# Products of k and v in column halves, one run of forty a batch, in a linear-attention, gated-attention and MLP kernel

## The chip, the cores and the metric

The kernel runs on one core of one Trainium2 chip. The metric is device time in microseconds of one execution; the kernel before was run three times. Its engines are named as in the profile: PE (TensorE), DVE (VectorE), ACT (ScalarE), POOL (GpSimd), SP (the queue that issues most DMAs).

## What is computed

Three stages follow one another for 8 batches of 576 positions, in f32. The change is in the first, a linear attention with 8 heads of 64 columns and a root-mean-square norm:

```python
kv = np.einsum('bhsd,bhse->bhde', k, v)
out = np.einsum('bhsd,bhde->bhse', q, kv)
rms = np.sqrt(np.mean(out * out, axis=-1, keepdims=True) + 1e-06)
return (out / rms * g_norm).astype(np.float32)
```

Its output, 512 wide, is the input x of the second stage: 4 experts of 64 columns, of which a gate picks two for each position. Each expert takes `q = x @ wq[e]`, `k = x @ wk[e]`, `v = x @ wv[e]`, causal softmax scores, `a @ v @ wo[e]`. The third stage is an MLP with a gelu, a layer norm and a product over positions:

```python
h = x @ w_in
h = 0.5 * h * (1.0 + np.tanh(c * (h + 0.044715 * h ** 3)))
...
v_s = np.einsum('ts,bsd->btd', w_sg, v_n) + b_sg[None, :, None]
gated = u * v_s
return (x + gated @ w_out).astype(np.float32)
```

## The kernel before

**Stages.** `Phase1` holds the first two stages, `Phase2` the MLP. For each batch `b`, Phase1 has six streams of work, each a generator:

- `front(b)`, the linear attention. Heads are handled in four pairs `c`, 128 columns wide. `kv` multiplies all 128 columns of k of a pair with all 128 of v, over five blocks of positions (three of 128, two of 96), into a PSUM bank `kvps`; the two 64x64 blocks on the diagonal are the heads' own, and ACT (upper) and DVE (lower) copy these into one of two f32 tiles `bd`, which were set to zero once. `outT` multiplies `bd` with q (two halves of 288 positions, `outps`); ACT copies the result to `o32` (named `o` in the trace) and POOL squares it (`sq`); in batch 0 DVE copies and ACT squares. `stat` sums the squares by head (`statps`, four column strips of 32), `rstd` makes the inverse root from it: ACT writes `ya` with a logarithm and an exponential, DVE refines it (`yb`, `yc`, `ya`), ACT and DVE split it (`yh`, `rr`).
- `normall(b)`: PE spreads `rr` over the columns (`nps`), DVE scales `o`, ACT rounds it to `xhi`, and DVE or POOL takes the rest `xlo`.
- `vpart(b)` (`vps`) and `qkpart(0, b)`, `qkpart(1, b)` (`qkps`): products with the weights, each in three terms of high and low parts.
- `attn(b)`: scores (`scps`), softmax (`prob`), transposes (`tps`, copied to `aT`), the product with v (`avps`, in two column halves of 64, `rps`), and its split `gav`, `gvh`, `gvl`.

Two more streams convert the MLP's weights (`cv_...` on DVE, ACT and POOL, and `wxps` on PE) and, at the start, split the weights of the projections (`wstage` into `whi` by ACT and `wlo` by POOL).

**Tiles.** In PSUM, four banks belong to `attn` (`psa`), three to all the rest of Phase1 (`psp`), one to `statps`. k, v and q of one pair are one load: three DMAs into a tile pair of the pool `ld`, which has `ldb` = 2 buffers; the loads of pairs 2 and 3 of batch 0 go to borrowed tiles (`kvmore`, `qmore`). `front` issues the load that takes a buffer over as soon as `kv` is recorded.

**The order.** The functions do not issue instructions; `Recorder` notes them. `merge` interleaves the streams: `OPT["w"]` gives each stream a start and an end in units of batches, and the number after each `yield` says how much of the stream is then done. `Recorder.plan` plays the recorded operations through a model of the engines, in which every engine takes the first ready operation in the merged order; `LAG` says how long a signal takes from one engine to another. `trace` then issues all operations in the order of their planned starts, all from line 453, so every row of the profile has that line. `together(ops)` marks matmuls that the plan must keep adjacent, and spreads their planned cost over the column tiles.

```python
def front(self, b, st):
    ...
    for c in range(NC):
        ops = self.kv(b, c)
        if b or c < 2:
            self.load(b * NC + c + (OPT["ldb"] if b else 2 + OPT["ldb"]))
        yield 1.1
        with self.hp("o"):
            sqs.append(self.outT(b, c, st, ops))
```

Of the kernel before, what the change touches and what calls it, by code (L numbers as in the profile page):

```python
# [27 lines left out]
F32 = mybir.dt.float32  # L28
F32R = mybir.dt.float32r
# [9 lines left out]
P = 128  # L39
S = 576  # L40
# [3 lines left out]
NC = 4  # L44
NQ = 5
HF = 288
BIG = 1.0e9
SMALL = float(np.array(897 << 20, np.uint32).view(np.float32))
OPT = dict(ob=1, sx=0, pinq=0, dv=0, pin=1, cvb=2, xb=1, ldb=2, hp={}, n1=0, n2=0, f1=0, pa=4, sA=(), dg=0, cost=(1.01, 0.88, 1.22, 1.47, 1.28), avi=1, prb=4, ahb=4, alb=2, qkb=2, ahead=3, w={'attn': (0.177, 1.304), 'qk1': (0.052, 0.235), 'qk0': (-0.558, 0.001), 'v': (-0.498, -0.304), 'front': (-1.553, -1.195), 'norm': (-0.834, -0.735), 'conv': (-0.409, 3.651), 'conv2': (3.099, 6.937), 'wts': (-1.719, -1.216), 'u': (-0.111, 1.169), 'front_0': (-1.826, -1.644), 'v_0': (-1.188, -0.934), 'qk0_0': (-1.196, -1.087), 'qk1_0': (0.028, 0.513), 'norm_0': (-1.552, -1.457)})

# [11 lines left out]
def _rows(i):  # L62

    return P if i < 3 else 96
# [5 lines left out]

LAG = {"tensor": 0.12, "vector": 0.13, "scalar": 0.13, "gpsimd": 0.13, "sync": 0.25, "dma": 0.12}
MODE = 0.15
# [389 lines left out]
class Phase1:  # L462
# [31 lines left out]
    def first_loads(self):  # L494

        nc = self.nc
        more = self.at.tile([P, 2, 2, NQ, P], F32, name="kvmore", tag="more", bufs=1)
        for n in range(NC):
            if n < 2:
                self.load(n)  # L500
            else:
                q = self.at.tile([P, S], F32, name="qmore", tag="prob", bufs=OPT["prb"])
                self.load(n, more[:, n - 2], q)
        for n in range(NC, NC + OPT["ldb"] - 2):
            self.load(n)
        self.stg = []
        for n0, n1 in ((512, 772), (0, 256), (256, 512)):
            st = self.staging(NC * (n1 - n0)).rearrange("p (c n) -> p c n", c=NC)
            nc.sync.dma_start(st, self.wqkvg.rearrange("(c p) n -> p c n", p=P)[:, :, n0:n1])
            self.stg.append(st)  # L510
# [4 lines left out]

    def load(self, n, kv=None, q=None):
        b, c = divmod(n, NC)
        if b >= self.nb:
            return
        nc = self.nc  # L520
        if kv is None:
            kv = self.ld.tile([P, 2, NQ, P], F32, name="kv", tag="kv")
            q = self.ld.tile([P, S], F32, name="q", tag="q")
        src = self.kvp[b, c]
        nc.sync.dma_start(kv[:, :, 0:3, :], src[:, 0:384].rearrange("t (p j) d -> p t (j d)", j=3))
        nc.sync.dma_start(kv[:96, :, 3:5, :], src[:, 384:S].rearrange("t (p j) d -> p t (j d)", j=2))
        nc.sync.dma_start(q, self.qT[b, c * P : (c + 1) * P, :])
        self.loads[n] = (q, kv[:, 0], kv[:, 1])

    def consts(self):  # L530
        nc, cst = self.nc, self.cst
# [12 lines left out]
        for j in range(E - 1):  # L544
            nc.gpsimd.memset(self.tri[:, :, j, j + 1 : E], 1.0)
        self.bd = []
        for i in range(2):
            t = cst.tile([P, P], F32, name=f"bd{i}")
            nc.vector.memset(t, 0.0)
            self.bd.append(t)  # L550
        self.rr = cst.tile([P, HF], F32R, name="rr")
# [31 lines left out]

    def kv(self, b, c):
        nc = self.nc
        q, k, v = self.loads[b * NC + c]
        ps = self.bank("kvps")
        for j in range(NQ):
            n = _rows(j)
            nc.tensor.matmul(ps[:, 0:P], k[:n, j, :], v[:n, j, :], start=(j == 0), stop=(j == NQ - 1))  # L590
        bd = self.bd[c % 2]
        nc.scalar.copy(bd[0:64, 0:64], ps[0:64, 0:64])
        nc.vector.tensor_copy(bd[64:128, 64:128], ps[64:128, 64:128])
        return bd, q

    def outT(self, b, c, st, ops):

        nc = self.nc
        bd, q = ops
        sq = self.tmp.tile([P, S], F32, name="sq", tag="sq", bufs=NC)  # L600
        for h in range(2):
            r = slice(HF * h, HF * (h + 1))
            ps = self.bank("outps")[:, 0:HF]
# [6 lines left out]
        if b:  # L610
            o = st["o32"][:, c, :]
# [17 lines left out]
    def rstd(self, st):  # L629
        nc = self.nc  # L630
# [7 lines left out]
        nc.vector.scalar_tensor_tensor(y, a, 1.5, y, op0=OP.add, op1=OP.mult)  # L638
        yh = self.tmp.tile([P, HF], F32R, name="yh", tag="yd")
        nc.scalar.copy(yh, y)  # L640
# [98 lines left out]
    def front(self, b, st):  # L739
# [4 lines left out]
        sqs = []  # L744
        for c in range(NC):
            ops = self.kv(b, c)
            if b or c < 2:
                self.load(b * NC + c + (OPT["ldb"] if b else 2 + OPT["ldb"]))
            yield 1.1
            with self.hp("o"):  # L750
                sqs.append(self.outT(b, c, st, ops))
            yield 0.75
            if c > 0:
                yield 0.5
        self.stat(st, sqs)
# [267 lines left out]
    def streams(self):  # L1023
# [4 lines left out]
        for b in range(self.nb):  # L1028
            st = sts[b]
            for name, gen, total, out in (  # L1030
# [4 lines left out]
                ("norm", self.normall(b, st), 1.0, prep),  # L1035
                ("front", self.front(b, st), 9.4, prep),
            ):
# [405 lines left out]
```

## Time and profile before

| | us |
|---|---|
| median of three runs | 847.2 (846.85 to 847.46) |
| the profiled execution | 847.4 |
| its span on the core | 845.6 |
| PE, DVE, ACT, POOL busy in it | 811.3, 462.3, 398.0, 321.9 |

A busy share counts the time in which at least one instruction of the engine is in work. PE's matmuls overlap and their ends are modelled, so what a matmul costs is the distance from its start to the next one's, which the chain of waits gives: it follows the execution back from its last instruction, at each step to what released it or to the instruction ahead of it on its engine. Waits are listed by who waited for whom. A matmul in f32 stands as two instructions in the trace, and as one in the order of a built program.

### The profile page before, as it was taken

How to read it: one execution, taken by the hardware profiler on the slowest of the kernel's cores; microseconds unless marked ns; L12 is line 12 of the kernel's file. 1: busy time of each engine (PE TensorE's matmuls, PEld its weight loads, DVE VectorE, ACT ScalarE, POOL GpSimd, SP SyncE). 2: the span in 40 equal slices, each digit the busy share in tenths (PEclk: the TensorE clock that was granted, in tenths of full speed). 3: DMA queues.
4: the chain of work that ended last, by engine and by line, in shares of the span. 5: the costliest groups of instructions: out<-in, count | busy, mean ns of one | idle time of the engine just before them, and what ended most of it. 6: DMA issues, size and time to landing. Idle time of an engine off the chain costs nothing.

```text
span 845.6 us, 15457 instructions
## 1 busy us (share of the span) xinstructions
PE 811.3 (96%) x5496; PEld 722.2 (85%) x5496; DVE 462.3 (55%) x1274; ACT 398.0 (47%) x1048; POOL 321.9 (38%) x387
## 2 busy tenths in 40 slices
PE   6599999999999999999999699999999999999998
PEld 5498979889798898888987599898989899898996
DVE  2557567776664757868656767362544435341330
ACT  3446466575565666667666673422333223322110
POOL 1963645647343343886311424131213222120120
PEclk9699999999999999999999899999999999999999
DMA  9667757687567777856379380302102030101011
GB/s 303 185 190 200 200 142 206 173 216 214 145 180 198 188 202 216 229 157 166 96 181 307 122 289 1 105 2 102 30 26 81 26 106 13 38 13 51 14 38 63
DMA packets 77088, 114.42 MB, mean 135 GB/s; under 512 B 13265, under 2 KB 40593, under 8 KB 77010
## 3 DMA queue, kind: packets, MB, share of 16 engines
q1 hardware_dynamic: 76866, 112.90, 46.2%
q8 instruction: 44, 0.72, 0.4%
q0 software_dynamic: 144, 0.52, 0.2%
q14 instruction: 34, 0.28, 0.1%
HBM read 58.31 MB, written 26.77 MB: 101 GB/s over the span
## 4 chain that ended last, share of the span: by engine, by line
PE 84%; DVE 7%; POOL 3%; ACT 3%; issue 2%; DMA 1%; SPq 0%; ACTq 0%; POOLq 0%; DVEq 0%
PE ps L453 42%; PE qkps L453 10%; PE vps L453 7%; PE scps L453 5%; PE tps L453 4%; PE avps L453 4%; PE kvps L453 4%; PE outps L453 4%; PE wxps L453 2%; PE nps L453 1%; DVE ya L453 1%; DVE yb L453 1%; DVE prob L453 1%; DMA q<-in_qT 1%; PE statps L453 1%
## 5 line engine op out<-in xcount | busy, mean ns | idle before, releaser
L453 PE MATMUL ps<-wsh,vn 128*128 128x288 f32 x576 | 120.1, 295 | 0.0
L453 ACT ACTIVATE prob<-prob,small 128x128 f32<-128x128 f32 (+4 forms) x160 | 96.5, 604 | 33.2 <-DVE small L453 29.7
L453 PEld LDWEIGHTS ps<-wsh,vn 128*128 128x128 f32 x576 | 94.3, 188 | 0.6
L453 POOL TENSOR_TENSOR gl<-g,gh 128x512 fp32r<-128x512 f32 x32 | 41.2, 1288 | 140.4 <-ACT gh L453 140.4
L453 PE MATMUL qkps<-xhi,whi 128*128 128x288 f32 x256 | 78.8, 308 | 1.4 <-DVE o L453 1.4
L453 DVE CUSTOM_DVE_ANT_0 prob<-scps,mask_sb 128x128 f32<-128x128 f32 (+4 forms) x160 | 73.8, 474 | 6.1 <-PE scps L453 5.3
L453 PE MATMUL qkps<-xlo,whi 128*128 128x288 f32 x256 | 77.0, 301 | 0.0
L453 PE MATMUL qkps<-xhi,wlo 128*128 128x288 f32 x256 | 76.6, 299 | 0.0
L453 PE MATMUL ps<-wsl,vn 128*128 128x288 f32 x256 | 75.5, 295 | 0.0
L453 PE MATMUL tps<-id_sb,prob 96*128 96x96 f32 (+2 forms) x480 | 71.2, 259 | 3.6 <-ACT aT L453 2.6
L453 PE MATMUL scps<-kh,qs 128*128 128x128 f32 (+2 forms) x192 | 67.3, 355 | 4.0 <-DVE aT L453 2.1
L453 POOL TENSOR_SCALAR lny<-mv 128x1 f32<-128x1 f32 x36 | 24.3, 674 | 120.5 <-DVE mv L453 120.4
L453 PE MATMUL scps<-kl,qs 128*128 128x128 f32 (+2 forms) x192 | 59.8, 314 | 0.0
L453 PEld LDWEIGHTS tps<-id_sb,prob 96*128 96x128 f32 (+2 forms) x480 | 52.0, 139 | 8.7 <-ACT aT L453 3.6
L453 ACT CAST gh<-g 128x512 fp32r<-128x512 f32 x32 | 19.9, 621 | 78.6 <-DVE g L453 60.9
L453 POOL TENSOR_TENSOR xlo<-o,xhi 128x576 fp32r<-128x576 f32 (+1 forms) x32 | 42.9, 1352 | 34.1 <-ACT xhi L453 27.3
L453 DVE TENSOR_TENSOR g<-ps,u 128x288 f32<-128x288 f32 x64 | 28.6, 451 | 41.9 <-PE ps L453 41.9
L453 PEld LDWEIGHTS qkps<-xhi,whi 128*128 128x128 f32 x256 | 48.7, 190 | 2.4 <-issue 1.7
L453 PE MATMUL ps<-wo2h,gl 128*128 128x512 f32 x128 | 50.1, 391 | 0.0
L453 PE MATMUL ps<-wo2l,gh 128*128 128x512 f32 x128 | 50.0, 391 | 0.0
L453 PE MATMUL ps<-wo2h,gh 128*128 128x512 f32 x128 | 49.9, 390 | 0.0
L453 PEld LDWEIGHTS qkps<-xlo,whi 128*128 128x128 f32 x256 | 48.9, 191 | 0.4
(174 smaller groups left out, 2214.1 us busy)
## 6 DMA issues: line engine op xcount, KB each, us to landing
kv<-in_kvp SPq DMA_DIRECT2D x30, 384.0 KB, 4.6
kh<-hiT SPq DMA_DIRECT2D x64, 144.0 KB, 2.9
kl<-loT SPq DMA_DIRECT2D x64, 144.0 KB, 2.9
q<-in_qT SPq DMA_DIRECT2D x30, 288.0 KB, 4.2
out<-oev SPq DMA_DIRECT2D x32, 256.0 KB, 2.0
kv<-in_kvp SPq DMA_DIRECT2D x30, 192.0 KB, 4.8
qs<-hiT SPq DMA_DIRECT2D x32, 144.0 KB, 2.5
qs<-loT SPq DMA_DIRECT2D x32, 144.0 KB, 2.6
```

The lines of the kernel that those rows point to most:

```text
L453: f(*[val(v) for v in op.args], **{k: val(v) for k, v in op.kw.items()})
```

## The change

- `kv(b, cs)` works on a list of pairs. It makes one product for each head: 64 columns of k by 64 of v, written to partitions 0 to 63 or 64 to 127 of the same columns of one bank. For four pairs that is 40 matmuls, and `together` keeps them adjacent. One ACT copy and one DVE copy move the blocks of all pairs in the list into one tile `bd` of four blocks.
- `front` calls it with all four pairs, but in batch 0 pair by pair. A load follows each `outT`, four pairs ahead.
- `ldb` is 4; the borrowed tiles and the special case in `first_loads` are gone; `yh` shares `yb`'s buffer.
- `LAG` is 0.2 us for PE, DVE, ACT and POOL, and several windows of `OPT["w"]` have other numbers. Both move the planned order everywhere in Phase1.

```diff
-LAG = {"tensor": 0.12, "vector": 0.13, "scalar": 0.13, "gpsimd": 0.13, "sync": 0.25, "dma": 0.12}
+LAG = {"tensor": 0.2, "vector": 0.2, "scalar": 0.2, "gpsimd": 0.2, "sync": 0.25, "dma": 0.12}
...
-        more = self.at.tile([P, 2, 2, NQ, P], F32, name="kvmore", tag="more", bufs=1)
-        for n in range(NC):
-            if n < 2:
-                self.load(n)
-            else:
-                q = self.at.tile([P, S], F32, name="qmore", tag="prob", bufs=OPT["prb"])
-                self.load(n, more[:, n - 2], q)
-        for n in range(NC, NC + OPT["ldb"] - 2):
+        for n in range(OPT["ldb"]):
             self.load(n)
...
-        self.bd = []
-        for i in range(2):
-            t = cst.tile([P, P], F32, name=f"bd{i}")
-            nc.vector.memset(t, 0.0)
-            self.bd.append(t)
+        self.bd = cst.tile([P, NC, P], F32, name="bd")
+        nc.vector.memset(self.bd, 0.0)
...
-    def kv(self, b, c):
-        nc = self.nc
-        q, k, v = self.loads[b * NC + c]
-        ps = self.bank("kvps")
-        for j in range(NQ):
-            n = _rows(j)
-            nc.tensor.matmul(ps[:, 0:P], k[:n, j, :], v[:n, j, :], start=(j == 0), stop=(j == NQ - 1))
-        bd = self.bd[c % 2]
-        nc.scalar.copy(bd[0:64, 0:64], ps[0:64, 0:64])
-        nc.vector.tensor_copy(bd[64:128, 64:128], ps[64:128, 64:128])
-        return bd, q
+    def kv(self, b, cs):
+        nc = self.nc
+        ps = self.bank("kvps")[:, 0:256].rearrange("p (c d) -> p c d", c=NC)
+        ops = []
+        for c in cs:
+            _, k, v = self.loads[b * NC + c]
+            for j in range(NQ):
+                n = _rows(j)
+                for r in (slice(0, 64), slice(64, 128)):
+                    ops.append(nc.tensor.matmul(ps[r, c], k[:n, j, r], v[:n, j, r], start=(j == 0), stop=(j == NQ - 1)))
+        nc.together(ops)
+        r = slice(cs[0], cs[-1] + 1)
+        nc.scalar.copy(self.bd[0:64, r, 0:64], ps[0:64, r])
+        nc.vector.tensor_copy(self.bd[64:128, r, 64:128], ps[64:128, r])
...
-        yh = self.tmp.tile([P, HF], F32R, name="yh", tag="yd")
+        yh = self.tmp.tile([P, HF], F32R, name="yh", tag="yb")
...
-        for c in range(NC):
-            ops = self.kv(b, c)
-            if b or c < 2:
-                self.load(b * NC + c + (OPT["ldb"] if b else 2 + OPT["ldb"]))
-            yield 1.1
-            with self.hp("o"):
-                sqs.append(self.outT(b, c, st, ops))
-            yield 0.75
-            if c > 0:
-                yield 0.5
+        for cs in [(c,) for c in range(NC)] if b == 0 else [range(NC)]:
+            self.kv(b, cs)
+            yield 0.6 * len(cs)
+            for c in cs:
+                sqs.append(self.outT(b, c, st))
+                self.load(b * NC + c + OPT["ldb"])
+                yield 1.0
```

In the `OPT` line `ldb=2` becomes `ldb=4`, and of the windows, `qk0`, `v`, `conv`, `conv2`, `wts`, `u` and those of batch 0 are moved by up to 0.3 of a batch. The weights after `front`'s yields change with its steps, and its total in `streams` from 9.4 to 6.9.

What the planned order makes of it, at three places. A row is an instruction with its output and inputs, "x40" forty alike in a row; a number behind a name is that of a buffer.

**PE inside a batch of the attention stage.** Before, at the first product of a batch's `kv`:

```order
L453 MATMUL qkps<-xhi,wlo 128x288
L453 MATMUL kvps<-kv 128x128 x5
L453 MATMUL tps<-id_sb,prob 128x96 x4
L453 MATMUL tps<-id_sb,prob 96x96
L453 MATMUL scps<-kh_2308,qs_1962 96x512
L453 MATMUL scps<-kl_2320,qs_1962 96x512
L453 MATMUL outps<-q,bd_87 128x288 x2
L453 MATMUL vps<-whi,xhi 128x260
```

After, at the same place:

```order
L453 MATMUL scps<-kh_2264,qs_2045 128x384
L453 MATMUL scps<-kl_2272,qs_2045 128x384
L453 MATMUL kvps<-kv 64x64 x40
L453 MATMUL tps<-id_sb,prob 128x96 x4
L453 MATMUL tps<-id_sb,prob 96x96
L453 MATMUL scps<-kh_2264,qs_2045 96x512
L453 MATMUL scps<-kl_2272,qs_2045 96x512
L453 MATMUL vps<-whi,xhi 128x260
```

The five matmuls of the first pair are replaced by the forty of all four; the three other groups of five, which stood further on between `vps` and `qkps` work, are gone, and the first `outps` has moved further back.

**ACT and DVE in the start.** ACT before, from the last pair of batch 0 on (`whi` are the casts of the projections' weights, `sq` the squares):

```order
L453 ACTIVATE sq<-outps 128x288 x2
L453 COPY bd_89<-kvps 64x64
L453 ACTIVATE sq<-outps 128x288 x2
L453 CAST whi<-wstage 128x260 x4
L453 CAST whi<-wstage 128x256 x7
L453 ACTIVATE ya<-statps,eps 128x288
L453 ACTIVATE ya<-ya 128x288
L453 CAST whi<-wstage 128x256
L453 COPY bd_87<-kvps 64x64
L453 CAST yh<-ya 128x288
```

ACT after:

```order
L453 ACTIVATE sq<-outps 128x288 x2
L453 COPY bd<-kvps 64x64
L453 CAST whi<-wstage 128x260 x4
L453 ACTIVATE sq<-outps 128x288 x2
L453 CAST whi<-wstage 128x256 x7
L453 ACTIVATE ya<-statps,eps 128x288
L453 ACTIVATE ya<-ya 128x288
L453 CAST whi<-wstage 128x256
L453 CAST yh<-ya 128x288
```

The four casts of the first part now stand ahead of the last pair's squares, and the copy of a batch 1 block between the last cast and `yh` is gone. DVE before, from that block's copy on:

```order
L453 COPY bd_87<-kvps 64x64
L453 TENSOR_SCALAR yc<-ya,side 128x288
L453 SCALAR_TENSOR_TENSOR rr<-yh,side,yc 128x288
L453 SCALAR_TENSOR_TENSOR o_164<-o_164,g_sb,nps 128x288 x2
L453 TENSOR_TENSOR xlo<-o_164,xhi 128x288
L453 SCALAR_TENSOR_TENSOR o_164<-o_164,g_sb,nps 128x288
L453 TENSOR_SCALAR cv_x_332<-cv_w 128x256
L453 SCALAR_TENSOR_TENSOR o_164<-o_164,g_sb,nps 128x288
L453 SCALAR_TENSOR_TENSOR cv_h<-cv_w,cv_x_332 128x256
L453 TENSOR_TENSOR xlo<-o_164,xhi 128x288
L453 SCALAR_TENSOR_TENSOR o_164<-o_164,g_sb,nps 128x288 x2
L453 TENSOR_SCALAR cv_h<-cv_x_332 128x256
```

DVE after, from the refined `ya` on:

```order
L453 SCALAR_TENSOR_TENSOR ya<-yb,ya 128x288
L453 TENSOR_SCALAR yc<-ya,side 128x288
L453 SCALAR_TENSOR_TENSOR rr<-yh,side,yc 128x288
L453 SCALAR_TENSOR_TENSOR o_168<-o_168,g_sb,nps 128x288 x3
L453 TENSOR_TENSOR xlo<-o_168,xhi 128x288
L453 SCALAR_TENSOR_TENSOR o_168<-o_168,g_sb,nps 128x288 x2
L453 TENSOR_TENSOR xlo<-o_168,xhi 128x288
L453 SCALAR_TENSOR_TENSOR o_168<-o_168,g_sb,nps 128x288 x2
L453 TENSOR_TENSOR xlo<-o_168,xhi 128x288
L453 SCALAR_TENSOR_TENSOR o_168<-o_168,g_sb,nps 128x288
L453 TENSOR_SCALAR cv_x_382<-cv_w 128x256
L453 TENSOR_TENSOR xlo<-o_168,xhi 128x288
```

The copy to `bd` is gone, and the conversion steps (`cv_x`, `cv_h`) that stood between the eight scalings of `o` stand behind them.

**DVE around `rstd` of a later batch.** `ISA prob` is the masked row minimum of scores, `ISA small` its read-out. Before, from the row sums on:

```order
L453 TENSOR_SCALAR yb<-statps 128x288
L453 TENSOR_TENSOR gav<-gav,rps 128x256
L453 TENSOR_TENSOR gav<-gav,rps 128x320
L453 TENSOR_TENSOR yc<-ya 128x288
L453 SCALAR_TENSOR_TENSOR yb<-yc,yb 128x288
L453 ISA prob,small<-scps,mask_sb 128x128
L453 ISA small 128x1
L453 SCALAR_TENSOR_TENSOR ya<-yb,ya 128x288
L453 TENSOR_TENSOR loT<-qkps,hiT 128x288
L453 TENSOR_SCALAR yc<-ya,side 128x288
L453 COPY aT_2261<-tps 128x3x128
L453 SCALAR_TENSOR_TENSOR rr<-yh,side,yc 128x288
```

After:

```order
L453 TENSOR_SCALAR yb<-statps 128x288
L453 TENSOR_TENSOR gav<-gav,rps 128x256
L453 TENSOR_TENSOR gav<-gav,rps 128x320
L453 TENSOR_TENSOR yc<-ya 128x288
L453 ISA prob,small<-scps,mask_sb 128x128
L453 ISA small 128x1
L453 SCALAR_TENSOR_TENSOR yb<-yc,yb 128x288
L453 COPY aT_2331<-tps 128x3x128
L453 SCALAR_TENSOR_TENSOR ya<-yb,ya 128x288
L453 ISA prob,small<-scps,mask_sb 128x256
L453 ISA small 128x1
L453 TENSOR_SCALAR yc<-ya,side 128x288
```

The two steps that refine `yb` and `ya` now have an `aT` copy between them, so that this copy stands ahead of `ya` in place of behind it; the copy of `loT` that stood there is elsewhere.

## Rows read from the trace of the kernel before

**Rows 1.** The page: busy time, share of the span and instructions of each engine.

```profile
PE 811.3 (96%) x5496; PEld 722.2 (85%) x5496; DVE 462.3 (55%) x1274; ACT 398.0 (47%) x1048; POOL 321.9 (38%) x387
```

**Rows 2.** Stretches of the span, PE alone: us, PE busy, granted clock, DMA share, GB/s.

```profile
0.00:40.00 40.00, 23.94 (x105) 0.83 0.83 251
...
330.00:385.00 55.00, 53.17 (x416) 1.00 0.67 186
...
500.00:846.00 346.00, 341.83 (x1981) 1.00 0.15 48
...
26.40:43.50 17.10, 11.78 (x39) 0.50 0.46 131
```

**Rows 3.** PE's waits: who for whom, us in total, times, longest us.

```profile
PE tps L453 <- ACT aT L453: 2.6, 4, 0.7
PE scps L453 <- DVE aT L453: 2.1, 3, 0.9
```

**Rows 4.** Chain that ended last, batches 3 and 4: start us, us, what.

```profile
154.20 1.14 PE kvps L453 x10
...
157.41 0.97 PE outps L453 x4
...
160.03 2.91 PE avps L453 x28
162.94 1.15 PE statps L453 x16
...
190.81 1.11 PE kvps L453 x10
```

**Rows 5.** Timeline near 126 us, PE; then PE's groups by form (last column: idle).

```profile
125.77 0.66 PE L453 MATMUL avps<-aT,vst 96*64 96x192 f32 x8
...
L453 PE MATMUL avps<-aT,vst 96*64 96x96 f32 x64 | 5.7, 245 | 0.0
```

**Rows 6.** Stretch with the most PE instructions in 2.3 us, columns as in rows 2.

```profile
378.80:381.10 2.30, 2.30 (x32) 1.00 0.03 7
```

**Rows 7.** Timeline of the start, PE: start us, us, instruction, count, [idle before <-releaser].

```profile
21.71 1.35 PE L453 MATMUL kvps<-kv 128*128 128x128 f32 x10 [0.20 <-PE statps L453]
29.72 1.33 PE L453 MATMUL outps<-q,bd 128*128 128x288 f32 x2 [6.65 <-DVE bd L453]
...
38.70 0.58 PE L453 MATMUL qkps<-xhi,whi 128*128 128x288 f32 x1 [1.38 <-DVE o L453]
```

**Rows 8.** Start: ACT, POOL timelines; loads of wstage (ns, first and last start, landing).

```profile
17.83 0.21 ACT L453 COPY bd<-kvps 64x64 f32<-64x64 f32 x1 [0.76 <-PE kvps L453]
...
19.93 1.33 ACT L453 CAST whi<-wstage 128x260 fp32r<-128x260 f32 x4
...
20.48 0.73 POOL L453 TENSOR_TENSOR wlo<-wstage,whi 128x260 fp32r<-128x260 f32 x1 [17.79 <-ACT whi L453]
...
L453 SPq DMA_DIRECT2D wstage<-in_wqkvg x3: 368/378/379, 9.4 to 11.5; - x3
...
DMA to landing us min/median/max: 7.5/8.3/8.7
```

**Rows 9.** Timeline of the start, DVE and (last row) ACT, as rows 7.

```profile
29.43 0.23 DVE L453 COPY bd<-kvps 64x64 f32<-64x64 f32 x1 [0.22 <-ACT bd L453]
...
31.90 0.99 DVE L453 SCALAR_TENSOR_TENSOR o<-o,g_sb,nps 128x288 f32<-128x288 f32 x2 [0.94 <-PE nps L453]
...
38.05 0.93 DVE L453 SCALAR_TENSOR_TENSOR o<-o,g_sb,nps 128x288 f32<-128x288 f32 x2
...
41.25 0.40 ACT L453 COPY o<-outps 128x288 f32<-128x288 f32 x1 [1.81 <-POOL xlo L453]
```

**Rows 10.** Timelines of DVE and PE in batch 4; eight ya by tile, min/median/max ns.

```profile
222.41 1.53 DVE L453 SCALAR_TENSOR_TENSOR ya<-yb,ya 128x288 f32<-128x288 f32 x1
...
224.84 0.38 PE L453 MATMUL tps<-id_sb,prob 96*128 96x96 f32 x2 [0.75 <-ACT aT L453]
...
L453 DVE SCALAR_TENSOR_TENSOR ya<-yb,ya x8: 459/1397/1531, 28.8 to 385.0; 128x288 f32<-128x288 f32 x8
```

More of the change, by code (lines that the diff above doesn't have):

```diff
@@ L48 @@
 SMALL = float(np.array(897 << 20, np.uint32).view(np.float32))
-OPT = dict(ob=1, sx=0, pinq=0, dv=0, pin=1, cvb=2, xb=1, ldb=2, hp={}, n1=0, n2=0, f1=0, pa=4, sA=(), dg=0, cost=(1.01, 0.88, 1.22, 1.47, 1.28), avi=1, prb=4, ahb=4, alb=2, qkb=2, ahead=3, w={'attn': (0.177, 1.304), 'qk1': (0.052, 0.235), 'qk0': (-0.558, 0.001), 'v': (-0.498, -0.304), 'front': (-1.553, -1.195), 'norm': (-0.834, -0.735), 'conv': (-0.409, 3.651), 'conv2': (3.099, 6.937), 'wts': (-1.719, -1.216), 'u': (-0.111, 1.169), 'front_0': (-1.826, -1.644), 'v_0': (-1.188, -0.934), 'qk0_0': (-1.196, -1.087), 'qk1_0': (0.028, 0.513), 'norm_0': (-1.552, -1.457)})
+OPT = dict(ob=1, sx=0, pinq=0, dv=0, pin=1, cvb=2, xb=1, ldb=4, hp={}, n1=0, n2=0, f1=0, pa=4, sA=(), dg=0, cost=(1.01, 0.88, 1.22, 1.47, 1.28), avi=1, prb=4, ahb=4, alb=2, qkb=2, ahead=3, w={'attn': (0.177, 1.304), 'qk1': (0.052, 0.235), 'qk0': (-0.631, -0.034), 'v': (-0.498, -0.468), 'front': (-1.553, -1.195), 'norm': (-0.834, -0.735), 'conv': (-0.532, 3.653), 'conv2': (2.801, 6.802), 'wts': (-1.719, -1.234), 'u': (-0.339, 0.941), 'front_0': (-1.733, -1.703), 'v_0': (-1.21, -0.923), 'qk0_0': (-1.183, -0.856), 'qk1_0': (0.099, 0.394), 'norm_0': (-1.303, -1.273)})
 AFTER = {
@@ L514, in staging, with load @@
         return self.at.tile([P, n], F32, name="wstage", tag="aT1", bufs=OPT["ahb"])
-    def load(self, n, kv=None, q=None):
+    def load(self, n):
         b, c = divmod(n, NC)
@@ L520, in load @@
         nc = self.nc
-        if kv is None:
-            kv = self.ld.tile([P, 2, NQ, P], F32, name="kv", tag="kv")
-            q = self.ld.tile([P, S], F32, name="q", tag="q")
+        kv = self.ld.tile([P, 2, NQ, P], F32, name="kv", tag="kv")
+        q = self.ld.tile([P, S], F32, name="q", tag="q")
         src = self.kvp[b, c]
@@ L581, in hp, with outT @@
         return self.tc.high_priority(offset=n) if n else nullcontext()
-    def kv(self, b, c):
+    def kv(self, b, cs):
         nc = self.nc
-        q, k, v = self.loads[b * NC + c]
-        ps = self.bank("kvps")
-        for j in range(NQ):
-            n = _rows(j)
-            nc.tensor.matmul(ps[:, 0:P], k[:n, j, :], v[:n, j, :], start=(j == 0), stop=(j == NQ - 1))
-        bd = self.bd[c % 2]
-        nc.scalar.copy(bd[0:64, 0:64], ps[0:64, 0:64])
-        nc.vector.tensor_copy(bd[64:128, 64:128], ps[64:128, 64:128])
-        return bd, q
-    def outT(self, b, c, st, ops):
+        ps = self.bank("kvps")[:, 0:256].rearrange("p (c d) -> p c d", c=NC)
[10 more added lines that the diff above has]
+        nc.vector.tensor_copy(self.bd[64:128, r, 64:128], ps[64:128, r])
+    def outT(self, b, c, st):
         nc = self.nc
-        bd, q = ops
+        bd, q = self.bd[:, c, :], self.loads[b * NC + c][0]
         sq = self.tmp.tile([P, S], F32, name="sq", tag="sq", bufs=NC)
@@ L1035, in streams @@
                 ("norm", self.normall(b, st), 1.0, prep),
-                ("front", self.front(b, st), 9.4, prep),
+                ("front", self.front(b, st), 6.9, prep),
             ):
```

## The prediction

> **What bounds the kernel now.** I began with the page: TensorE (PE) is busy for 96% of the span [rows 1]. A busy PE need not be a PE at its peak, so the second view was the stretches. In the attention stage one batch takes 55 us, and even the loosest of these stretches has PE busy for all but 1.8 us, at the full granted clock; the long last stretch is busy for 98%. The first 40 us are different: 23.9 us busy, and part of them at half the clock [rows 2]. The third view, PE's waits, shows what recurs behind the start: a small wait, once a batch, on copies of transposed scores [rows 3]. So from 40 to 455 us an edit pays by what it takes off PE's own queue; before that, by what it takes off the chain of the other engines. The stage behind the attention is not touched.
>
> **The products of k and v.** The fourth view is the chain of waits. Each pair of heads costs PE ten matmul instructions in 1.11 to 1.14 us (five blocks of rows, two passes each for f32), four times a batch: 4.49 us [rows 4]. Half of what they compute, the blocks that mix two heads, is thrown away.
>
> After the change a step is two 64-column halves that write different partitions; there are forty such steps a batch (20 blocks of rows by two passes), in one run. To price a step I take two sizes from the chain [rows 4]: four instructions of 288 columns in 0.97 us (0.2425 each), ten of 128 in 1.11 (0.111 each). The line through them is 5.8 ns plus 0.822 ns a column, so 64 columns take 58.4 ns. That the halves run side by side is seen in the attention product, whose 28 instructions work in the same column halves: each half streams 2 x 1632 = 3264 columns, by the line 2.76 us, and the row says 2.91 us for both halves together [rows 4]. The rest, 0.15 us, is the turn into and out of this way of working; the row sums, in four column strips, leave 1.15 - 0.97 = 0.18. I take 0.17. The block then costs 40 x 0.0584 + 0.17 = 2.51 us in place of 4.49: **-1.98 us a batch**.
>
> The line is proven down to 96 columns: the last eight instructions of the attention product (two steps of 192, one of 96, then the last pair's own 0.245) take 0.66 us, so 0.415 for 480 columns, where the line says 0.412 [rows 5]. What no row shows is 64. Bounds: at best the line; next, a step that goes no faster than the 96-column one (0.082 us, so 3.45 us a block, a gain of 1.04); at worst the two halves go one behind the other (0.117 us, 4.85 us, a loss of 0.36). I take the line, since its 96-column point is nearest and loads two halves of 64 columns already.
>
> One thing else is new: 80 instructions in 2.3 us, 29 ns each. The densest 2.3 us that I found holds 32, 72 ns each [rows 6], and these were set by their columns, not by how fast they came. [...] The sum stays with the line.
>
> Batches 2 to 7 have the full gain: 6 x 1.98 = **-11.9**. Batch 1 has less, because one of its four products stands at 21.71 us today, and half of one product with q at 29.72, both in time that PE idles anyway [rows 7]; now all stand in the dense stretch. Before: 3 x 1.12 = 3.36; after: 2.51 + 2 x 0.2425 = 3.00; **-0.4**. Batch 0 is in the start, below. The copies of the blocks fall from four a batch on each of ACT and DVE to one wide one: worth nothing, as neither engine bounds. A block now waits for the last of its four loads. Its buffer comes free with the last product of the batch before with q, which ends at 158.4 us where the next batch's products begin at 190.81 [rows 4]: 32 us of cover, against 8.7 us for the slowest landing in [rows 8]. If it went, each us late would be a us of PE.
>
> **The start, 20 to 39 us.** PE's dense work begins at 38.70 us, released by DVE [rows 7], and the chain back from there runs through POOL's splitting of the weights, which began at 20.48 when ACT had cast their first part, at 19.93 [rows 8]. ACT's casts stood behind two squares of the last pair. The new order has the casts ahead of these. The weights' first part lands at 9.4 + 7.5 = 16.9 us at the earliest, and the copy ahead of the casts ends at 18.04 [rows 8]. So POOL starts between 17.5 (the landing decides) and 18.6 (the copy stays where it is): -1.9 to -3.0. I take -2.3, since shorter products bring the copy forward a little. The same POOL and ACT instructions then follow up to rr, all earlier by that. Next, the copies of a batch 1 block leave the queues between ya and rr: DVE's alone is 0.22 us idle and 0.23 work [rows 9]; -0.4. Then, from the first o (31.90) to the one that released PE (about 38.52), DVE needed 6.6 us for seven o, three xlo and four conversion steps [rows 9]. In the new order no conversion step stands among the first eight o. And a PSUM bank of batch 1, held until ACT's copy at 41.25 [rows 9], is free, so three banks turn over in place of two and the sixth o is enough: six o and two xlo, an xlo (same width) priced as an o, 8 x 0.465 = 3.7, so -2.9. Sum -5.6. Against it stands the clock: PE idled from 23.1 us [rows 7] and had the lower level, 1.2 GHz, from 26.4 to 43.5 us [rows 2]; the idle stretch begins earlier now, and each us of dense work at that level costs half a us. I take **-5.0**, bounds -1.5 (a gate that I missed, conversions late elsewhere) and -6.5.
>
> **The stall once a batch.** At 222.41 DVE's ya takes 1.53 us beside POOL's gvl; the shortest of the eight takes 0.46 [rows 10]. Behind it in DVE's queue stand loT, yc and the copy aT, and PE's next transposes wait 0.75 us. Seven such waits sum to 4.7 us (2.6 + 2.1) [rows 3]. The new order puts one aT copy ahead of ya. What follows ya can still be late, so I take two thirds: **-3.0**, bounds 0 and -4.7. The wider allowances for signals (0.2 us for 0.12 and 0.13) and the new windows move the rest of the lists; PE has 1 to 1.8 us of idle time a batch, most of it this stall, so I give them no term, but up to -4 in the range.
>
> **The sum.** The profiled execution took 847.4 us, 0.2 above the median. 847.4 - 11.9 - 0.4 - 5.0 - 3.0 = 827.1; forecast 827 us.
>
> **Rivals.**
> - *The halves overlap in part*: steps of 0.082 us. Batches 2 to 7 gain 6.2, batch 1 loses 0.6 (3.45 + 0.49 - 3.36), start and stall as above: 833.8. For it: nothing shorter than 96 columns is in the trace. Against: the line fits there to 3 ns in 415.
> - *The change does not do what it says*: halves one behind the other, 0.117 us a step. 6 x 0.36 + 2.0 lost, 8.0 gained: 843.6. Against it: the 2.91 us of [rows 4].
> - *Instructions come too slowly*: PE takes them no faster than its densest stretch shows, 72 ns. A block costs 80 x 0.072 + 0.17 = 5.9; six batches lose 1.4 each, batch 1 loses 3.1; with 8.0 gained elsewhere 851, **slower**. It decides from 65 ns an instruction, where 560 of these instructions eat all gains. For it: no row shows a faster run of that length. Against: the stretch in [rows 6] had columns to stream all the time. [...]
>
> **How the numbers follow.** Forecast 0.65 (its own bounds 820 to 834: start at -6.5, the whole stall and the 4 us; or start at -1.5 and no stall gain), partial overlap 0.18 (834 to 841 in the same way), one behind the other 0.08, too slow 0.06, and 0.03 for a new wait of another kind. The range 820 to 841 leaves out the last three, 0.17. A measurement can tell about 0.2% (1.7 us) from no change. Faster: 0.65 + 0.18 + most of 0.08; what is left of that and a part of the slow cases count as the same. That gives 0.88, 0.05, 0.07.
>
> **What would show it.** Right: the chain of waits has one block of 80 kvps instructions of about 2.3 us a batch; the first dense PE row stands near 33 to 34 us; from one block to the next it is about 53 us where it is 55; the stretch behind the change of stage is as long as now (some 346 us). Wrong: kvps blocks of 3.3 us or more; POOL's first wlo still at 20 us; a wait of PE on kv loads or on bd; transposes still waiting 0.7 us on aT; or a longer change of stage.

## The result and the profile after

The changed kernel takes **826.27 us** (median of 4 runs, 825.42 to 828.0), the kernel before 847.33 us in the same comparison: a ratio of 0.9754, 95% interval 0.9735 to 0.9773. The forecast was 827.0, the range 820 to 841. The profiled execution took 827.08 us with a span of 825.2; the span before was 845.6, so 20.4 us are to be placed.

The page and three stretches of PE, for [rows 1, 2] (us, PE busy, granted clock, DMA share, GB/s):

```profile
PE 796.0 (96%) x5816; PEld 702.6 (85%) x5816; DVE 453.5 (55%) x1252; ACT 395.1 (48%) x1027; POOL 323.7 (39%) x387
```

```profile
34.00:40.00 6.00, 5.50 (x44) 1.00 0.32 93
280.00:332.00 52.00, 51.41 (x465) 1.00 0.81 217
500.00:825.00 325.00, 321.42 (x1846) 1.00 0.14 46
```

PE's share is 96% as before. A kernel can become 20 us shorter with its bound as busy as it was: there was less for PE to do, and the rest moved up. The first row is the start: PE already works at full clock (1.00) where the kernel before had the half clock (0.50) [rows 2].

**The block.** The chain of waits, batch 3, for [rows 4] (start us, us, what):

```profile
127.63 2.48 PE kvps L453 x80
...
181.83 2.48 PE kvps L453 x80
```

All seven blocks read 2.48 us. Such a row goes from the end of the group ahead to the end of the group itself, not from start to start, as the section on the time before has it. What a block costs is seen only together with its neighbours, in the timeline of PE (start us, us, instruction, count; a duration runs into the next row, as 49.05 + 0.29 is past 49.27):

```profile
49.05 0.29 PE L453 MATMUL qkps<-xhi,wlo 128*128 128x288 f32 x1
49.27 2.55 PE L453 MATMUL kvps<-kv 128*64 128x64 f32 x80
51.75 0.40 PE L453 MATMUL qkps<-xhi,whi 128*128 128x288 f32 x1
51.99 0.29 PE L453 MATMUL qkps<-xlo,whi 128*128 128x288 f32 x1
```

Two such qkps elsewhere follow each other by 0.13 (48.92 and 49.05, for one). Here the block starts 0.22 after the one ahead of it, and the one behind it takes 0.24 to its successor. From 49.05 to 51.99 are 2.94; less 0.13 for each of the two qkps, the block costs PE 2.68. The seven blocks give 2.62 to 2.68 in this way, 2.65 in the mean. The kernel before, two of the four pairs of batch 3:

```profile
135.38 1.28 PE L453 MATMUL kvps<-kv 128*128 128x128 f32 x10
136.49 0.49 PE L453 MATMUL tps<-id_sb,prob 96*128 96x96 f32 x4
...
154.03 1.31 PE L453 MATMUL kvps<-kv 128*128 128x128 f32 x10
155.09 0.38 PE L453 MATMUL qkps<-xhi,whi 128*128 128x288 f32 x1
155.31 0.29 PE L453 MATMUL qkps<-xlo,whi 128*128 128x288 f32 x1
```

From start to start these pairs read 1.11 and 1.06. But the qkps behind the second one takes 0.22 to its successor, where 0.13 is usual, and these 0.09 belong to the pair: 1.15. In this way the four pairs add up to the 4.49 of the chain's rows [rows 4]. A block costs PE 1.84 less than the four pairs.

**The waits of PE** on work of the attention stage, first of the changed kernel (100 to 420 us), then of the kernel before (105 to 420 us); in total, times, longest:

```profile
PE scps L453 <- DVE small L453: 1.2, 4, 0.5
PE outps L453 <- DVE loT L453: 0.6, 1, 0.6
PE scps L453 <- DVE aT L453: 0.3, 1, 0.3
PE qkps L453 <- DVE o L453: 0.2, 1, 0.2
```

```profile
PE tps L453 <- ACT aT L453: 2.6, 4, 0.7
PE scps L453 <- DVE aT L453: 1.9, 2, 0.9
PE scps L453 <- DVE gav L453: 0.9, 2, 0.5
PE tps L453 <- DVE small L453: 0.4, 2, 0.2
PE tps L453 <- DVE aT L453: 0.4, 1, 0.4
```

2.3 us in place of 6.2. The waits on aT are all but gone. From the first dense row of PE to its last avps, before and after (columns as in the stretches above):

```profile
38.70:471.60 432.90, 425.30 (x3288) 0.99 0.69 191
34.91:452.54 417.63, 413.34 (x3584) 1.00 0.73 197
```

Over this whole part of the execution PE idles for 4.3 us in place of 7.6.

**The start**, timelines of the changed kernel (PE, ACT, POOL and DVE; in brackets the idle time before and who ended it):

```profile
15.53 2.29 PE L453 MATMUL outps<-q,bd 128*128 128x288 f32 x4 [0.57 <-DVE bd L453]
...
19.24 1.34 ACT L453 CAST whi<-wstage 128x260 fp32r<-128x260 f32 x4
...
19.79 1.42 POOL L453 TENSOR_TENSOR wlo<-wstage,whi 128x260 fp32r<-128x260 f32 x2 [17.10 <-ACT whi L453]
...
31.13 1.48 DVE L453 SCALAR_TENSOR_TENSOR o<-o,g_sb,nps 128x288 f32<-128x288 f32 x3 [0.96 <-PE nps L453]
...
34.27 0.93 DVE L453 SCALAR_TENSOR_TENSOR o<-o,g_sb,nps 128x288 f32<-128x288 f32 x2
...
34.91 0.36 PE L453 MATMUL vps<-whi,xhi 128*128 128x260 f32 x1 [0.50 <-DVE o L453]
```

The dense work begins at 34.91 in place of 38.70 us, but POOL's first wlo at 19.79 in place of 20.48 [rows 7, 8]: the start is shorter, in part by other steps than forecast. The first o begins at 31.13 in place of 31.90 [rows 9], and the sixth, which released PE, ends near 34.8: 3.6 us of DVE, where it took 6.6 before.

**Sum of the profiles.** The dense work begins 3.8 us earlier, the part up to the last avps is 15.3 shorter (417.6 in place of 432.9), and the rest up to the end 1.3 (372.7 in place of 374.0). Of the 15.3, the blocks of batches 2 to 7 are 6 x (4.49 - 2.65) = 11.0 and the idle time 3.3. The kernel before ran its dense work at half the clock from 38.70 to 43.5 us [rows 2, 7], the changed kernel none of it: half of 4.8 is another 2.4 (an estimate). Batch 1 gives 0.2 by the forecast's reckoning with 2.65 for the block. Against it stand 0.9 us for four products of the MLP (`ps`) that now come ahead of the last avps; that work is missing from the rest. These come to 16.0; 0.7 stays open.

| us | forecast | measured |
|---|---|---|
| blocks of batches 2 to 7 | -11.9 | -11.0 |
| batch 1 | -0.4 | -0.2 |
| the start with its clock | -5.0 | -3.8 - 2.4 = -6.2 |
| idle time in the attention | -3.0 | -3.3 |
| the rest | 0 | -1.3 + 0.9 = -0.4 |
| sum | -20.3 | -21.1; the spans differ by -20.4 |

### The profile page after: what moved, and what is told of

Its sections match the earlier page's. It is cut to its first block, busy times and chain, and to the rows that moved or that the text cites. A ratio compares the mean times of both kernels' runs of the same rounds, so it can differ in the third digit from the quotient of the medians.

```text
span 825.2 us, 16042 instructions
## 1 busy us (share of the span) xinstructions
PE 796.0 (96%) x5816; PEld 702.6 (85%) x5816; DVE 453.5 (55%) x1252; ACT 395.1 (48%) x1027; POOL 323.7 (39%) x387
## 4 chain that ended last, share of the span: by engine, by line
PE 84%; DVE 6%; DMA 4%; ACT 2%; issue 2%; SPq 1%; POOL 1%; DVEq 0%; ACTq 0%; POOLq 0%
PE ps L453 43%; PE qkps L453 10%; PE vps L453 7%; PE scps L453 5%; PE avps L453 5%; PE outps L453 4%; PE tps L453 4%; PE kvps L453 3%; PE wxps L453 2%; DMA xl<-gvl 1%; PE nps L453 1%; SPq L453 1%; PE statps L453 1%; DMA wsl<-wd1l 1%; DMA q<-in_qT 1%
## 5 line engine op out<-in xcount | busy, mean ns | idle before, releaser
L453 DVE CUSTOM_DVE_ANT_0 prob<-scps,mask_sb 128x128 f32<-128x128 f32 (+4 forms) x160 | 74.8, 475 | 10.5 <-PE scps L453 9.5
L453 ACT ACTIVATE vn<-vg,lny 128x512 fp32r<-128x512 f32 x32 | 23.1, 725 | 57.1 <-POOL lny L453 55.6
```

Of the source, the lines that this page charges most:

```text
L453: f(*[val(v) for v in op.args], **{k: val(v) for k, v in op.kw.items()})
```

## The experiments

The first question was whether the halves carry the gain, or the new order list.

**Full width again, still adjacent.** The order of all other instructions is that of the changed kernel.

```diff
+        if b > 0:
+            return self.kv_full(b, cs)
...
+                ops.append(nc.tensor.matmul(ps[:, c], k[:n, j, :], v[:n, j, :], start=(j == 0), stop=(j == NQ - 1)))
```

> The changed kernel, with the products of k and v of batches 1 to 7 at full width again (20 instructions of 128 columns, all four pairs adjacent in one bank), and the same order of everything else. Theory (column halves that run side by side carry the gain): a block takes about 20 x 0.111 x 2 passes as in the kernel before, 4.4 to 4.5 us in place of 2.48, so the whole is 7 x 2.0 = 14 us above the changed kernel, about 840 us, less where idle time of PE took some of it (836 to 842). Rival (the new order list, buffers and signals carry the gain, the halves little): no more than 3 us above the changed kernel, 826 to 829.

Measured: 839.73 us, 0.9909 of before (0.9892 to 0.9927), 13.5 above the changed kernel: the theory. The chain of waits shows why:

```profile
76.94 4.48 PE kvps L453 x40
131.80 4.46 PE kvps L453 x40
```

7 x (4.47 - 2.48) = 13.9 by these rows. The whole part from the first dense row to the last avps, with the same list:

```profile
35.21:465.30 430.09, 425.72 (x3303) 1.00 0.71 192
```

PE is busy 12.4 us longer here than in the changed kernel (413.34), 1.77 a block. So a block in halves costs 4.46 - 1.77 = 2.69, and 0.2 of that stands in the row of what follows, not in its own 2.48. Given this list, the halves carry nine tenths of what they were said to carry.

**One half after the other.** The loop over the halves is moved outside.

```diff
-        for c in cs:
-            _, k, v = self.loads[b * NC + c]
-            for j in range(NQ):
-                n = _rows(j)
-                for r in (slice(0, 64), slice(64, 128)):
+        for r in (slice(0, 64), slice(64, 128)):
+            for c in cs:
+                _, k, v = self.loads[b * NC + c]
+                for j in range(NQ):
+                    n = _rows(j)
```

> The changed kernel, with all 40 instructions of the upper column half of a batch first and then all 40 of the lower one, in place of halves that alternate. Theory (two halves overlap only where their instructions stand next to each other): a block takes 80 x 0.0584 = 4.7 us in place of 2.48, and the whole is 7 x 2.2 = 15 us above the changed kernel, about 841 us. Rival (the queue looks ahead over 40 instructions, or the time is set by columns in all): the same time as the changed kernel, within 1 us.

Measured: 846.08 us, 0.9987 of before (0.9976 to 0.9998), 19.8 above the changed kernel; nearly all that the change brings is gone. Timeline of PE:

```profile
131.20 0.34 PE L453 MATMUL scps<-kl,qs 128*128 128x384 f32 x1
131.47 4.00 PE L453 MATMUL kvps<-kv 128*64 128x64 f32 x68
135.92 0.91 PE L453 MATMUL kvps<-kv 96*64 96x64 f32 x12 [0.46 <-ACT bd L453]
136.76 0.30 PE L453 MATMUL tps<-id_sb,prob 96*128 96x96 f32 x1
```

From 131.47 to 136.76 is 5.29 us: 80 x 0.0584 = 4.67, and about 0.6 for a wait that this version adds. The theory had 4.7 and no such wait. With the upper half done first, the list puts ACT's copy of it amid the block, and the instruction behind it waits for the copy. 7 x (5.29 - 2.48) = 19.7. So two halves overlap where their instructions alternate (2.48 us) and not in this order (5.29), and an instruction of 64 columns by itself takes some 58 ns here (68 of them in 4.00 us).

**Halves in the kernel before, pair by pair.** Twenty instructions in place of ten, kept together, the list planned anew:

```diff
+        if b > 0:
...
+                for r in (slice(0, 64), slice(64, 128)):
+                    ops.append(nc.tensor.matmul(ps[r, 0:64], k[:n, j, r], v[:n, j, r], start=(j == 0), stop=(j == NQ - 1)))
+            nc.together(ops)
```

> The kernel before, with the products of batches 1 to 7 in column halves, pair by pair as they stood (10 instructions become 20 of 64 columns, next to each other; the list is planned anew with the pairs kept whole). Theory (a block of one pair costs 10 steps of 0.0584 us and 0.17 us for the turn into and out of the halves): 0.75 us a pair in place of 1.12, so 1.47 us a batch, and 6 x 1.47 + 1.1 = 10 us below the kernel before, 836 to 839 us. Rival (the turn costs much more than 0.17 us, so that only the adjacency of all four pairs makes it pay): a pair takes 1.0 us or more, and the whole is within 3 us of the kernel before.

Measured: 846.28 us, 0.9987 of before (0.9974 to 1.0). The chain has what the theory wanted of a pair, but the time hardly moved:

```profile
62.80 0.73 PE kvps L453 x20
```

The list had changed too: the dense work begins at 39.27 us in place of 38.70, and PE's waits from 105 to 420 us are 6.7 us in place of 6.2. By the time this is the rival. So the list was taken out of the comparison.

**The same with the list of the kernel before, instruction for instruction.** Each product instruction is given out as two when the list is already set.

```diff
+            if b > 0:
+                op.fn = "halves"
...
+            if op.fn == "halves":
+                o, x, y = [val(v) for v in op.args]
+                for r in (slice(0, 64), slice(64, 128)):
+                    tc.nc.tensor.matmul(o[r, r], x[:, r], y[:, r], start=op.kw["start"], stop=op.kw["stop"])
+                continue
```

> The kernel before with its order list kept exactly, each product instruction of batches 1 to 7 given out as two of 64 columns (pairs apart, as they stood). Theory (halves alone are worth their columns, and what went missing in the run before went into the new list): a pair takes 0.73 us in place of 1.12, 0.39 x 24 = 9.4 us in batches 2 to 7 and about 1 us in batch 1 (where pairs are cut by other work and turn more often), so about 10 us below the kernel before, 836 to 839 us. Rival (a gap elsewhere on PE takes the gain back even in the same order, as the copies of the blocks then come too late for the products with q): 842 us or more.

Measured: 844.29 us, 0.9966 of before (0.9952 to 0.998): 3.5 us, a third of what was expected. Here a size was wrong, that of the turn. Timeline of PE:

```profile
133.51 0.29 PE L458 MATMUL qkps<-xhi,wlo 128*128 128x288 f32 x1
133.73 0.80 PE L455 MATMUL kvps<-kv 128*64 128x64 f32 x20
134.47 0.63 PE L458 MATMUL tps<-id_sb,prob 96*128 96x96 f32 x5
```

The first gap is 0.22 where these instructions otherwise follow each other by 0.13, so the turn into the halves is 0.09 us; from its start to the start of what follows the pair takes 0.74; and the next full-width instruction loses another 0.06 to 0.11. Together 0.9, against 1.12 at full width: a gain of 0.22 a pair and not 0.39. In each of batches 5 to 7 other work cuts one pair in two, and such a pair gains nothing; that leaves 4.4 us in six batches. As one adjacent block the work of four pairs is 2.65 where four pairs apart are 3.6. So of the 1.84 us a batch that the changed kernel gains, about 1.0 is the adjacency: three turns saved, at some 0.32 each. The part from the first dense row to the last avps:

```profile
37.92:467.60 429.68, 420.73 (x3557) 1.00 0.69 193
```

PE is busy 4.6 us less than before (425.30). It idles 1.4 more (9.0 in place of 7.6); the dense work begins 0.8 earlier, and the rest behind the last avps takes 1.0 more (375.0 in place of 374.0). That makes 3.0, the whole difference of the two profiles (842.6 and 845.6).

The second question was the start.

**Full width in batch 0 alone**, as in the first experiment with the condition turned round, and **halves in batch 0 alone of the kernel before**, as in the last one with its condition turned round:

```diff
+        if b == 0:
+            return self.kv_full(b, cs)
```

> The changed kernel, with full-width products in batch 0 alone, where PE waits for loads anyway; the order is the same. Theory (in the changed kernel the clock stays at 1.2 GHz up to 23.4 us because the shorter products leave PE idle more, which makes the products with q 2.29 us in place of 1.24 and puts the last copy into bd at 19.13 us in place of 17.83): the clock rises near 12.8 us again, the four outps take 1.2 to 1.3 us, the last copy comes 0.5 to 1.3 us earlier, and the dense work begins up to 1 us earlier, where the clock may be lower then; the whole is 825 to 827 us. Rival (the clock in the first 20 us decides nothing, POOL and DVE do): the rows of the start shift but the first dense PE row stands at 34.9 us within 0.3, and the whole is the same within 1 us. Third case: the clock rises at 12.8 us but then falls for the dense start, as in the kernel before (low up to 43.5 us): 2 to 4 us slower than the changed kernel.

> The kernel before with its order list kept exactly, the products of batch 0 alone in halves. Theory (the shorter products keep PE too little busy in the first 20 us, so that the clock stays at 1.2 GHz there and rises only later): no rise of the clock near 12.8 us, the products with q of batch 0 at 2.2 to 2.4 us in place of 1.24, the last copy into bd about 1 us later and POOL's first wlo up to 1 us later; if the clock is then high in the dense start, as in the changed kernel, the 43.5 us up to which it was low come down and the whole is 0 to 3 us shorter (844 to 847), if not, 0 to 1 us longer. Rival (the clock of the start follows from something else in the change, the four load buffers or the order): the clock rises at 12.8 us and falls at 26.4 us as before, and the whole is the same within 0.5 us.

Measured: 825.38 us, 0.9745 of before (0.9724 to 0.9765), for the first, with the dense work at 32.94 us; 846.74 us, 1.0 of before (0.9985 to 1.0016), for the second. The first looked like the theory, and like a faster kernel. In the second one's profile the theory held step by step: two of the three later groups of products with q take 2.29 us, the granted clock is first on record at 19.1 us (12.8 before), POOL's first wlo stands at 21.75 and the dense work begins at 39.97. Its time did not change. So the changed kernel and its version with full-width products in batch 0 were run again, side by side.

> The changed kernel itself once more, beside the next run on the same chip, as the measure for it: 825 to 828 us, and a profile whose clock in the first 35 us need not be the one shown (high from 23.4 to 26.9 us), if that differs from run to run.

> The changed kernel with full-width products in batch 0 alone, once more, timed in more runs. Theory (the full-width products bring the clock up at about 11 us, and POOL's splitting with it 2 us forward, in most runs): 1 to 2 us below the changed kernel beside it, POOL's first wlo near 17.8 us. Rival (the rise of the clock in the start differs from run to run for either kernel, so that the 2.0 us between the two profiles were chance): the same within 0.5 us.

Measured: the changed kernel 825.11 us (0.9741 of before, 0.9725 to 0.9758), the other 825.75 us (0.9745, 0.9731 to 0.9759). No difference clear of the noise, and the theory falls as far as the time goes: the profiles of one and the same kernel differ. Timelines of the changed kernel in its second profile:

```profile
16.33 1.24 PE L453 MATMUL outps<-q,bd 128*128 128x288 f32 x4 [0.57 <-DVE bd L453]
...
16.77 1.34 ACT L453 CAST whi<-wstage 128x260 fp32r<-128x260 f32 x4 [0.76 <-DMA wstage<-in_wqkvg]
...
17.32 2.80 POOL L453 TENSOR_TENSOR wlo<-wstage,whi 128x260 fp32r<-128x260 f32 x4 [14.63 <-ACT whi L453]
...
32.44 0.36 PE L453 MATMUL vps<-whi,xhi 128*128 128x260 f32 x1 [0.50 <-DVE o L453]
```

The four products with q take 1.24 us where they took 2.29 above, ACT's cast now follows the landing of the weights and not the last copy, POOL starts 2.5 us earlier, and so does the dense work. The span is 822.4 in place of 825.2. The kernel with full-width products in batch 0 had it the other way round, early in its first profile and late in its second, POOL's first wlo:

```profile
17.83 2.82 POOL L453 TENSOR_TENSOR wlo<-wstage,whi 128x260 fp32r<-128x260 f32 x4 [15.14 <-ACT whi L453]
```

```profile
20.63 2.83 POOL L453 TENSOR_TENSOR wlo<-wstage,whi 128x260 fp32r<-128x260 f32 x4 [17.94 <-ACT whi L453]
```

The granted clock has no record there before it first rises (at 23.4 us in the first profile of the changed kernel, at 10.5 in the second), and the doubled time of the products with q (2.29 us for 1.24) agrees with the lower level until then; on record, as from 26.9 to 33.6 us in that first profile, this level is 0.50 of the full clock. When the clock rises in the start differs from run to run of one kernel. That it is no part of the change is not shown, however. In the six kept profiles with full-width products in batch 0 the first record stands at 10.8 to 16.9 us; in the seven with alternating halves there it is twice near 10 (10.1 and 10.5) and five times at 18.9 to 23.5. So the halves may well make a late rise more frequent; in the times of the changed kernel and its version with full-width products in batch 0 it does not show.

In the changed kernel neither the halves of batch 0 nor the new windows and allowances (below) are needed for the early dense start. What is left is the list with the four buffers and the copies that left the queues, as the forecast had it; these were not tried one by one.

The third question was the list: what the wider allowances for signals and the new windows are worth, which the forecast gave no term.

**The old allowances, the old windows, and both**, each in the changed kernel:

```diff
-LAG = {"tensor": 0.2, "vector": 0.2, "scalar": 0.2, "gpsimd": 0.2, "sync": 0.25, "dma": 0.12}
+LAG = {"tensor": 0.12, "vector": 0.13, "scalar": 0.13, "gpsimd": 0.13, "sync": 0.25, "dma": 0.12}
```

> The changed kernel with the old allowances for signals (0.12 and 0.13 us in place of 0.2) in what plans its order list. Theory (the slack is worth little: PE has 1 to 1.8 us of idle time a batch in the kernel before, most of it one stall): within 2 us of the changed kernel, 825 to 829. Rival (the slack is what removed the stall once a batch and brought the start forward): 3 to 6 us slower, 829 to 832.

Measured: 831.36 us (0.9804 of before, 0.9772 to 0.9835), some 5 above the changed kernel, though its four runs spread from 827.15 to 833.01 and the profile is of the shortest. By the median this is the rival.

The next text names the old allowances as well; the kernel that ran has the windows (w in OPT) of the kernel before and kept the new allowances:

> The changed kernel with the old windows and the old allowances for signals in what plans its order list, so that of the change only the products, the buffers and the order that follows from them are left. Theory (products 12 us, and the start mostly from the freed queues): 827 to 832. Rival (the tuned windows carry the start and the stall, 6 us and more): 833 us or more.

Measured: 832.08 us (0.9819, 0.9796 to 0.9843). The text's ranges were meant for both old values and do not judge this run.

> The changed kernel with the old windows and the old allowances for signals in what plans its order list: of the change, the products in halves, the adjacent block, the four buffers and the list that follows from them. Theory (allowances and windows each remove the same few waits on the copies of the transposed scores and the gated values, so that losing both costs little more than losing one): 831 to 835 us. Rival (they add up, some 5 us each): 836 us or more.

Measured: 836.39 us (0.9883, 0.9857 to 0.9908): the rival, they add up. PE's waits from 100 to 420 us:

```profile
PE scps L453 <- DVE small L453: 2.4, 2, 1.8
PE tps L453 <- DVE small L453: 2.3, 2, 1.4
PE tps L453 <- ACT aT L453: 1.4, 2, 0.8
PE scps L453 <- DVE gav L453: 1.1, 1, 1.1
PE scps L453 <- DVE aT L453: 0.9, 1, 0.9
```

With two short ones (0.3 and 0.2) these are 8.6 us, in place of 2.3. And two of them, together, may have cost twice. Stretches of PE in the same kernel (columns as above):

```profile
155.50:159.00 3.50, 3.50 (x41) 1.00 0.20 50
159.00:162.20 3.20, 1.47 (x11) 1.00 0.11 36
162.30:165.60 3.30, 3.30 (x16) 0.50 0.58 161
```

PE idled for 1.7 of 3.2 us, waiting on gav and small, and then worked for 3.3 us at half the clock, which is another 1.7 us. This is one profile; that the idle time brought the fall of the clock is what the order of the rows suggests. The dense work begins at 34.88 us here, as in the first profile of the changed kernel: the windows and allowances are not what brings the start forward in it. 6.3 us of waits and 1.7 of clock are 8.0 of the 9.7 us between the two profiles (834.9 and 825.2).

**The new allowances in the kernel before**, that one line alone:

> The kernel before, with the new allowances for signals (0.2 us) alone. Theory (the wider allowances are worth something by themselves, because copies that the list takes to be there are late on the chip): 3 to 5 us below the kernel before, 842 to 845. Rival (a list is only as good as the windows that were chosen for it, and either change alone gives a list that was not chosen): the same or slower, 846 to 851.

Measured: 844.22 us, 0.9966 of before (0.9955 to 0.9977). The theory, by its number; but not by its reason: PE's waits in the attention are 5.7 us there (6.2 before), and it is the dense work that begins earlier, at 35.56 in place of 38.70 us: this list, too, has no conversion step among DVE's first seven o. The new windows and allowances together were not tried in the kernel before.

## Why the prediction was right

**The products: right mechanism, gain too large by 0.9 us.** The term that was mis-sized is the turn, "I take 0.17". The 4.49 holds, and so does the line: drawn through 288 and 128 columns, it is good at 64, where steps follow each other by 58 to 59 ns. Forty steps are 2.34 us; the block costs 2.65, so the turn is some 0.32: 0.09 ahead of the first instruction, 0.15 from the last one to the next full-width one, and the rest in that one. The forecast took it from two rows of the chain, and such a row ends with its own group: what the next full-width instruction loses is not in it. So -11.0 in place of -11.9. That the turn decides how the change must be made stood in no step: paid four times a batch, it leaves 0.86 of the 1.84 us.

**The rivals.** *Halves that overlap in part* and *one behind the other* are refuted by the 2.48 us; the second is what the version with one half after the other really does. *Instructions come too slowly* is refuted too: 80 instructions in 2.33 us from first to last start, 29 ns each, where that rival needed 65 ns or more.

**The start: -6.2 for -5.0, by steps that nearly cancel.** "POOL starts between 17.5 and 18.6" failed in the first profile (19.79, so -0.7 for -2.3) and was slightly exceeded in the second (17.32, when the landing decided, as the step said). The first o came 0.8 us earlier for a forecast of 2.7. DVE's six o in place of seven, with no conversion among them, held: 3.6 us for the 3.7 forecast. And the sign of the clock was wrong: "+0.6" for a dense start at the low level, where PE has the full level in both profiles (1.00 from 34 to 40 us in the first, from 31 to 37 in the second), which is worth an estimated 2.4 the other way. The forecast had some luck there.

**The stall: right by size (-3.3 for -3.0), incomplete on where it comes from.** The forecast read the earlier aT copy in the new list and then gave the allowances and windows "no term". But they make that list: with both old, the waits are 8.6 us, more than before the change, and the time 836.39. Put in order, the products, the buffers and the start are worth 11.0 us (847.4 to 836.4), the allowances and windows another 10 to 11 (836.4 to 825.1 or 826.3), which suggests that the old values had been chosen for the old products. The order of the steps matters, though: the new allowances alone are worth 3.1 us in the kernel before, and both new values were not tried there. The forecast had some 17 us for products and start together, and without the new values 11 are left: that was not seen.

**What would make it wrong** did not appear, except one: POOL's first wlo near 20 us, which I had named as a sign of a missed gate and which went with the clock: 19.79 us with its first record at 23.4, 17.32 with it at 10.5.

## What to carry to other kernels

Price a group of matmuls together with its neighbours: from the start of the instruction ahead to the start of the second one behind, less what those two take elsewhere. A row of the chain ends with the group and leaves out what the next instruction loses by a turn; the distance from start to start leaves it out too. A run that differs in this group alone settles it. Here work in column halves paid where the halves alternated (846.08 us with one after the other, 826.27 alternating), and most in one long block, because each turn into and out of it cost some 0.32 us. And where an order list is planned from costs, try its parameters anew with a shorter operation: with the old ones, 11 of the 21 us were left here. How much of the other 10 the old products would have had too was not tried.

## What the runs showed of the hardware

- The clock's rise in the first 25 us differs between runs of one kernel (first record at 23.4 and at 10.5 us in two profiles of the changed kernel), and POOL's first wlo behind it moved by 2.5 us there (19.79 and 17.32) and by 2.8 in the version with full-width products in batch 0 (17.83 and 20.63): two profiles of the same kernel are not equal there, and a difference of 2 us in a start is not yet an effect. Alternating halves in batch 0 went with a late rise (18.9 to 23.5 us) in five of seven profiles, full width in none of six (10.8 to 16.9).
- A wait within dense work was followed by a low clock once, in the changed kernel with the old windows and allowances: 1.7 us idle in 3.2 us, and then 3.3 us at a granted clock of 0.50.
- 64-column f32 instructions in alternating halves went at 29 ns each over 80 instructions (2.33 us from first to last start), two halves starting 6 to 7 ns apart.
- The turn into halves and back cost full-width work some 0.32 us: 0.09 ahead, 0.15 behind the last instruction, and 0.06 to 0.11 in the instruction that follows (0.24 us to its successor in place of 0.13).
